# Decode attention with a dense branch: the last head's output weights in two halves of the width, the sum in two banks

## The chip, the cores and the metric

One core of a Trainium2 chip. The metric is device time in microseconds (us). "Before" and "changed" are the two kernels.

In the lines of the profile, PE is the tensor engine (matmuls) and PEld its weight loads, DVE is VectorE, ACT ScalarE, POOL GpSimd, and SPq the queue of SyncE, which issues the transfers. A line of the timeline gives start and length in us, the engine, the line of the kernel and the operation; in brackets stand the idle time before it and what ended it. PSUM is the memory that matmuls write their sums to; a bank is one part of it. A transfer has landed when the last of its completion signals (16 for a load here) is recorded.

## The reference

Two branches are added to a residual: attention of 16 query heads over the last 4096 positions of a key and value cache of 8 heads, with an output projection, and a small dense layer.

```python
W = min(4096, max(256, Sk // 4))                 # 4096
q = (layernorm(x) @ wq)...                        # B=2, one position, 16 heads of 256
k = repeat(k_cache[:, :, Sk-W:, :], 2)            # 8 kv heads -> 16
scores = einsum("bhqd,bhkd->bhqk", q, k) * 256**-0.5
o = einsum("bhqk,bhkd->bhqd", softmax(scores), v)
return x + o.reshape(B, 1, 4096) @ wo + dense(layernorm(x))   # [2, 1, 448]
```

The cache slices and the weights make 77.66 MB. The arithmetic is small: the result is 2 rows of 448 values.

## The kernel before

The key and value caches stream in through one DMA queue, issued by SyncE. Each kv head's two query heads end in matmuls with 448 KB of output weights. The weights of the last kv head (query heads 14 and 15, 224 KB each) are the last thing loaded. From there on the sum lives in four column tiles of one PSUM bank, 112 columns each:

```python
NO, DO = 4, D // 4                                 # 4 pieces of 112 columns
psA = ps_a.tile([P, DO], FP32, name="psA")         # one bank; piece n in partitions 32n, 32n+1
def add_last(lhsT, w, start=False, stop=False):
    for n in range(NO):
        nc.tensor.matmul(part(n), lhsT=lhsT, rhs=w[:, n*DO:(n+1)*DO], tile_position=(0, n*Q), ...)
...
# loads of the last weights: one transfer per query head, rows of 1792 bytes per partition
win = A_wo[r0 : r0 + rep*Dh, :].rearrange("(h p c) d -> p h (c d)", h=rep, p=P)
...
for h in range(rep):                               # the last kv head
    for c in range(ND):                            # ND = 2 halves of the head's 256 values
        add_last(oT[:, c, h, :], w[:, h, c*D:(c+1)*D], ...)
...
for n in range(NO):                                # the end
    copy = nc.vector.tensor_copy if n // 2 == 0 else nc.scalar.copy
    copy(out=res[:, n*DO:(n+1)*DO], in_=part(n))
nc.sync.dma_start(out=out, in_=res[:])
```

The softmax here doesn't subtract the row's maximum and nothing guards it: scores larger than these inputs give would overflow.

Of the kernel before, what the change touches and what calls it, by code (L numbers as in the profile page):

```python
# [12 lines left out]
FP32 = mybir.dt.float32  # L13
# [21 lines left out]
def kernel(  # L35
# [13 lines left out]
    nc = tc.nc  # L49
    P = 128  # L50
    Q = 32
    NQ = P // Q

    Bsz, Sq, D = A_x.shape
    _, Hkv, Sk, Dh = A_k_cache.shape
    HqDh = A_wq.shape[1]
    Hq = HqDh // Dh
    rep = Hq // Hkv
# [14 lines left out]
    ND = Dh // P  # L73
# [21 lines left out]
    ps_a = ctx.enter_context(tc.tile_pool(name="ps_a", bufs=1, space=PSUM))  # L95
# [16 lines left out]
    for lo, hi in ((0, SC), (SC, NS)):  # L112
# [16 lines left out]
        out=rstd[:], in_=mv[:, 1:2], func=ACT.Sqrt, bias=eps_t[:], scale=1.0  # L129
# [5 lines left out]
    for r in range(2):  # L135
        n = (NS + 1 - r) // 2
        nc.vector.tensor_scalar(  # L137
            out=xn_bf[:, r : NS : 2, :, :],
# [12 lines left out]
    for j in range(1, NQ):  # L151
        nc.vector.tensor_tensor(
            out=hsel, in0=hsel, in1=ident[:, j * Q : (j + 1) * Q : HS], op=ALU.add
# [4 lines left out]
    for b in range(Bsz):  # L158
        nc.vector.tensor_reduce(
            out=off[:, b : b + 1], in_=hsel[:, b * rep : (b + 1) * rep], axis=AXIS.X, op=ALU.add  # L160
# [4 lines left out]
        out=off[:], in0=off[:], scalar1=mine[:], scalar2=1e4, op0=ALU.subtract, op1=ALU.mult  # L165
# [4 lines left out]
    for h in range(rep):  # L170
        nc.vector.tensor_reduce(
            out=own[:, :, h],
            in_=ident[:, h * PH : (h + 1) * PH].unsqueeze(1).to_broadcast([P, Bsz, PH]),
# [14 lines left out]
    for s in range(NS):  # L188
# [7 lines left out]
        out=odd[:],  # L196
        in_=ident[:].rearrange("p (u o) -> p o u", o=2),
# [4 lines left out]
    for par in range(2):  # L202
        for x in range(NX):
            which = (par + x) % 2
            nc.vector.tensor_scalar(
                out=xs[:, par : NS : 2, x, :],
# [3 lines left out]
                op0=ALU.mult,  # L210
            )

    psE = ps_a.tile([Bsz, D], FP32, name="psE")

    def add(lhsT, w, start=False, stop=False):
        nc.tensor.matmul(  # L216
            psE[:], lhsT=lhsT, rhs=w, start=start, stop=stop, skip_group_check=True
        )
# [2 lines left out]



    NO = NQ
    DO = D // NO
    psA = ps_a.tile([P, DO], FP32, name="psA")

    def part(n):
        return psA[n * Q : n * Q + Bsz, :]

    def add_last(lhsT, w, start=False, stop=False):
        for n in range(NO):
            nc.tensor.matmul(  # L233
                part(n),
                lhsT=lhsT,
                rhs=w[:, n * DO : (n + 1) * DO],
                start=start,
                stop=stop,
                tile_position=(0, n * Q),
                skip_group_check=True,  # L240
            )

    def carry():
        early = consts.tile([Bsz, D], FP32, name="early")
        nc.vector.tensor_copy(out=early[:], in_=psE[:])
        add_last(ident_f[0:Bsz, 0:Bsz], early[:, :], start=True)


# [29 lines left out]
    def build_q(i):  # L278
# [17 lines left out]
    nc.vector.tensor_copy(  # L296
        out=half[:], in_=ident[0:NX, 0:NX].unsqueeze(2).to_broadcast([NX, NX, Bsz])
    )
    NB1 = 5
    act_bf = consts.tile([P, NF, NX, Bsz], BF16)  # L300
    dense = {}

    def load_dense():
# [14 lines left out]
        b1_in = B_b1.rearrange("(x f) -> x f", x=NX)  # L318
        for u in range(NB1):
            cols = slice(u * HF // NB1, (u + 1) * HF // NB1)  # L320
            nc.scalar.dma_start(out=b1_sb[:, cols], in_=b1_in[:, cols])
# [59 lines left out]
    def load_k(i, cuts=(0, T)):  # L381
        k_t[i] = k_pool.tile([P, T * Dh], BF16, tag="k", name="k")
        load_cache(k_t[i], A_k_cache, i, cuts)

    def load_v(i, cuts=(0, T)):
        t = v_tile()
        load_cache(t, A_v_cache, i, cuts)
        v_t[i] = t[:].rearrange("p (t d) -> p t d", t=T)

    def load_wo(kvh, parts=1):  # L390
        w = wo_pool.tile([P, rep, ND * D], BF16, tag="wo", name="wo")
        r0 = kvh * rep * Dh
        wo_t[kvh] = w
        if kvh < Hkv - NFIX:

            nc.sync.dma_start(
                out=w[:].rearrange("p h n -> p (h n)"),
                in_=A_wo[r0 : r0 + rep * Dh, :].rearrange("(p j) d -> p (j d)", p=P),
            )
            return  # L400
        win = A_wo[r0 : r0 + rep * Dh, :].rearrange("(h p c) d -> p h (c d)", h=rep, p=P)
        for u in range(parts):
            hs = slice(u * rep // parts, (u + 1) * rep // parts)
            nc.sync.dma_start(out=w[:, hs, :], in_=win[:, hs, :])  # L404

    def turn(s):
        kt = kt_pool.tile([P, TH * Dh], BF16, tag="kt", name="kt")
        i, half = divmod(s, NH)
        k = k_t[i] if half < NH - 1 else k_t.pop(i)
        nc.vector.transpose(  # L410
            out=kt[:].bitcast(FP32),
            in_=k[:, half * TH * Dh : (half + 1) * TH * Dh].bitcast(FP32),
        )
        kt_t[s] = kt
# [31 lines left out]
    def turn_p(s):  # L446
        pT = p_pool.tile([P, TH * Q], BF16, tag="pT", name="pT", bufs=2 * NH + 1)
        nc.vector.transpose(out=pT[:], in_=p_t.pop(s)[:])  # L448
        pT_t[s] = pT
        i, half = divmod(s, NH)  # L450
        if half != NH - 1:
            return
        rs = state.pop(("rs", i))
        total = small.tile([P, 1], FP32, tag="total", name="total")
        nc.vector.tensor_reduce(out=total[:], in_=rs[:], axis=AXIS.XY, op=ALU.add)
        sums = small.tile([P, BR], FP32, tag="sums", name="sums")
        nc.vector.tensor_scalar(  # L457
            out=sums[:], in0=hsel, scalar1=total[:], scalar2=None, op0=ALU.mult
        )
        state["sums", i] = sums  # L460
# [75 lines left out]
    def finish(i):  # L536
        pqv = state.pop(("pq", i))
        rec = state.pop(("rec", i))

        o = small.tile([P, NJ, NP, BR], FP32, tag="osum", name="osum")  # L540
        for u in range(NP):
            nc.vector.tensor_tensor(
                out=o[:, :, u, :],
                in0=pqv[:, :, u, u * BR : (u + 1) * BR],
                in1=rec[:].unsqueeze(1).to_broadcast([P, NJ, BR]),
                op=ALU.mult,
            )
        oT = small.tile([P, NJ, Bsz], BF16, tag="oTm", name="oTm")
        with nc.allow_low_precision("sums of fp32 factors, rounded once"):
            nc.vector.tensor_reduce(  # L550
                out=oT[:],
                in_=o[:].rearrange("p j u (b h) -> p j b u h", b=Bsz),
                axis=AXIS.XY,
                op=ALU.add,
            )
        state["oT", i] = oT
# [22 lines left out]
    def mix(kvh):  # L579
        oT = state.pop(("oT", kvh))  # L580
        w = wo_t.pop(kvh)
        if kvh < Hkv - NFIX:
            for j in range(NJ):
                add(
                    oT[:, j, :],
                    w[:].rearrange("p h (c d) -> p (h c) d", c=ND)[:, j, :],
                    stop=(kvh == Hkv - NFIX - 1 and j == NJ - 1),
                )
            return
        for h in range(rep):  # L590
            for c in range(ND):
                add_last(
                    oT[:, c, h, :],
                    w[:, h, c * D : (c + 1) * D],
                    stop=(kvh == Hkv - 1 and h == rep - 1 and c == ND - 1),
                )

    load_k(0)
    load_dense()
# [4 lines left out]
    for i in range(Hkv + 1):  # L604
        if i + 1 < Hkv:
            load_k(i + 1, (0, T) if i + 1 < Hkv - 1 else (0, T // 2, T))
        if i < Hkv:
            load_v(i, (0, T) if i < Hkv - 1 else (0, T // 2, 13 * T // 16, 15 * T // 16, T))
            load_wo(i, parts=1 if i < Hkv - 1 else 2)
            for piece in range(NH):  # L610
                s = i * NH + piece
                if s + 1 < NSTEP:
                    turn(s + 1)
                if piece == 1 and i > 1:
                    finish(i - 2)
                scores(s)
                if i == Hkv - 1 and piece == 2:
                    carry()
                if s >= 1:
                    turn_p(s - 1)  # L620
                if s == NSTEP - 1:
                    turn_p(s)
                if piece == 0 and i > 1:
                    turn_o(i - 2)
                if piece == 1 and i > 1:
                    mix(i - 2)
            if i + 2 < Hkv:
                build_q(i + 2)
        else:
            mix(i - 2)  # L630
        if i == 0:
            dense_in()
            dense_out()
        if i >= 1:
            if i - 1 < Hkv - NFIX:
                values(i - 1)
            else:
                values_fixed(i - 1)
        if i == Hkv:
            mix(i - 1)  # L640

    res = consts.tile([Bsz, D], BF16)
    for n in range(NO):
        copy = nc.vector.tensor_copy if n // 2 == 0 else nc.scalar.copy
        copy(out=res[:, n * DO : (n + 1) * DO], in_=part(n))
    nc.sync.dma_start(out=out.flatten_outer_dims(), in_=res[:])
    issue_in_order(tc)
# [30 lines left out]
```

## Time and profile before

| | before |
|---|---|
| median of the first 3 runs | 189.32 us (189.31 to 189.41) |
| load queue busy | 97.0% of the span |
| PE / VectorE / ScalarE busy | 75% / 58% / 24% |
| last weights at PE | 184.56 us |
| store issued | 185.56 us |
| span of the profile | 187.6 us |

The span is counted from the first instruction profiled; the device time of that run, 189.44 us, is 1.9 us longer. Read the table from below: the store leaves 2 us before the end, the last weights reach PE 1 us before the store, and up to about 183 us the loads have kept the memory busy; then they run dry. The lines of the profile are in the prediction.

### The profile page before, as it was taken

The numbers are of one execution on the slowest core, as the hardware profiler recorded it, in microseconds if no ns is written. First come the engines' busy times: TensorE is split into PE (matmuls) and PEld (weight loads), VectorE is DVE, ScalarE is ACT, GpSimd is POOL, SyncE is SP. The second block draws the span as 40 slices with busy tenths as digits, with TensorE's granted clock in tenths as the row PEclk, the third lists the DMA queues.
The fourth block names the chain that finished last, engine by engine and source line by source line (L and its number), as shares of the span: only waits on it lengthen the run. The fifth ranks groups of instructions, "written<-read, shape, count | busy, mean of one in ns | idle before, by whom it ended". The sixth has DMA issues, their size and how long they took to land.

```text
span 187.6 us, 2418 instructions
## 1 busy us (share of the span) xinstructions
PE 140.9 (75%) x938; PEld 64.9 (35%) x938; DVE 108.6 (58%) x150; ACT 45.3 (24%) x148; POOL 16.3 (9%) x74
## 2 busy tenths in 40 slices
PE   0394099904989999956896769955995869999773
PEld 0141033801334434422342324421441324444672
DVE  6705497049671994079803992099506993995201
ACT  3005015200062144024222224033312233154001
POOL 7000500300003001100030003000120000000000
PEclk9999859965799999999999999999999999999655
DMA  6999899999999999999998999999999999999991
GB/s 228 414 477 440 378 429 444 447 444 447 433 419 426 407 420 445 433 447 390 484 446 384 426 433 440 433 447 421 446 437 426 390 438 426 451 444 398 415 395 43
DMA packets 5046, 77.81 MB, mean 415 GB/s; under 512 B 552, under 2 KB 1068, under 8 KB 2348
## 3 DMA queue, kind: packets, MB, share of 16 engines
q1 hardware_dynamic: 5012, 77.66, 97.0%
q8 instruction: 7, 0.11, 0.2%
q14 instruction: 3, 0.02, 0.0%
q10 hardware_dynamic: 24, 0.01, 0.0%
HBM read 77.67 MB, written 0.00 MB: 414 GB/s over the span
## 4 chain that ended last, share of the span: by engine, by line
DMA 66%; DVE 20%; PE 8%; SPq 2%; ACT 1%; issue 1%; ACTq 0%; DVEq 0%
DMA k<-in_A_k_cache_dram 57%; DVE kt L410 16%; DMA wo<-in_A_wo_dram 9%; PE sc L422 4%; PE o L490 4%; DVE pT L448 3%; SPq L379 2%; ACT p L436 1%; PE psE L216 0%; SPq L113 0%; DVE sums L457 0%; SPq L404 0%; DVE oTm L550 0%; DVE recm L482 0%; PE psA L233 0%
## 5 line engine op out<-in xcount | busy, mean ns | idle before, releaser
L410 DVE STREAM_TRANSPOSE kt<-k 128x2048 f32<-128x2048 f32 x32 | 73.3, 2295 | 51.8 <-DMA k<-in_A_k_cache_dram 51.8
L422 PE MATMUL sc<-kt,qdiag 128*128 128x512 bf16 x256 | 62.6, 389 | 19.7 <-DVE kt L410 18.9
L436 ACT ACTIVATE p<-sc,off 128x256 bf16<-128x256 f32 x64 | 33.0, 543 | 69.6 <-PE sc L422 69.0
L490 PE MATMUL o<-v,pT 128*8 128x512 bf16 x192 | 42.5, 379 | 0.0
L422 PEld LDWEIGHTS <-qdiag 128*128 128x128 bf16 x256 | 23.0, 98 | 55.7 <-issue 20.9
L490 PEld LDWEIGHTS <-pT 128*8 128x8 bf16 x192 | 17.2, 92 | 22.4
L448 DVE STREAM_TRANSPOSE pT<-p 128x512 bf16<-128x512 bf16 x32 | 21.8, 681 | 5.1 <-ACT p L436 5.1
L285 POOL COPY qdiag<-qt 32x16 bf16<-32x16 bf16 x64 | 12.9, 247 | 120.2 <-PE sc L422 104.2
L499 ACT COPY o_sb<-o 8x512 f32<-8x512 f32 x12 | 6.3, 572 | 36.3 <-PE o L490 36.3
L436 ACT ACTIVATION_READ_ACCUMULATOR p<-sc,off 128x1 f32 x64 | 11.7, 183 | 0.0
L216 PE MATMUL psE<-wo,oTm 128*2 128x448 bf16 x24 | 5.5, 351 | 6.5 <-DVE oTm L550 6.5
L216 PE MATMUL psE<-v,act_bf 128*2 128x448 bf16 x14 | 4.9, 533 | 7.0 <-DVE act_bf L360 7.0
L569 PE MATMUL q<-pT,v 128*128 128x4 bf16 x256 | 7.8, 169 | 2.4 <-DMA v<-in_A_v_cache_dram 2.1
L265 PE MATMUL q_ps<-v,xq 128*128 128x512 bf16 x28 | 7.5, 435 | 2.1 <-DVE xq L256 2.1
L569 PEld LDWEIGHTS <-v 128*128 128x128 bf16 x256 | 7.3, 101 | 3.4 <-DMA v<-in_A_v_cache_dram 3.3
L275 DVE CAST q_sb<-q_ps 128x512 bf16<-128x512 f32 x2 | 1.3, 686 | 7.0 <-PE q_ps L265 7.0
L265 PEld LDWEIGHTS <-xq 128*128 128x128 bf16 x28 | 3.0, 110 | 6.6 <-DVE xq L256 2.5
L216 PEld LDWEIGHTS <-oTm 128*2 128x2 bf16 x24 | 1.5, 82 | 10.7 <-DVE oTm L550 9.0
L216 PEld LDWEIGHTS <-act_bf 128*2 128x2 bf16 x14 | 1.6, 117 | 10.0 <-DVE act_bf L360 7.1
L189 PE MATMUL xnT_ps<-ident,xn_bf 2*128 2x2 bf16 x7 | 0.5, 166 | 5.7 <-DVE xn_bf L137 5.7
L529 PEld LDWEIGHTS q<-ident_f,o_sb 8*128 8x128 f32 x48 | 3.4, 136 | 2.5 <-issue 2.5
L529 PE MATMUL q<-ident_f,o_sb 8*128 8x8 f32 x48 | 3.9, 204 | 0.0
(60 smaller groups left out, 46.5 us busy)
## 6 DMA issues: line engine op xcount, KB each, us to landing
k<-in_A_k_cache_dram SPq DMA_DIRECT2D x7, 4096.0 KB, 26.9
v<-in_A_v_cache_dram SPq DMA_DIRECT2D x7, 4096.0 KB, 25.7
k<-in_A_k_cache_dram SPq DMA_DIRECT2D x2, 2048.0 KB, 28.8
v<-in_B_w_dram SPq DMA_DIRECT2D x2, 1568.0 KB, 17.0
wo<-in_A_wo_dram SPq DMA_DIRECT2D x7, 448.0 KB, 30.2
v<-in_A_wq_dram SPq DMA_DIRECT2D x1, 2048.0 KB, 7.4
v<-in_A_v_cache_dram SPq DMA_DIRECT2D x1, 2048.0 KB, 15.2
v<-in_A_wq_dram SPq DMA_DIRECT2D x1, 1536.0 KB, 10.8
```

The source lines that it names most:

```text
L216: nc.tensor.matmul(psE[:], lhsT=lhsT, rhs=w, start=start, stop=stop, skip_group_check=True)
L265: nc.tensor.matmul(ps[u][:], lhsT=xq[:, s, :, :].rearrange("p j k -> p (j k)"), rhs=wq_sb[:, s, u * N5 : (u + 1) * N5], start=(s == 0), st ...
L285: nc.gpsimd.tensor_copy(out=tv[rows, :, e, j * Q : (j + 1) * Q : HS].rearrange("p n (b h) -> p n b h", b=Bsz), in_=qv[rows, :, h0 : h0 + r ...
L379: nc.sync.dma_start(out=t[:, cols], in_=src[:, :, cols])
L410: nc.vector.transpose(out=kt[:].bitcast(FP32), in_=k[:, half * TH * Dh : (half + 1) * TH * Dh].bitcast(FP32),)
L422: nc.tensor.matmul(psc[:], lhsT=qdiag[i % NW][:, n * NE + e, :], rhs=ktv[:, n, e, :, :], start=(n == 0 and e == 0), stop=(n == NB - 1 and ...
L436: nc.scalar.activation(out=pv[:, b, :, :], in_=sv[:, b, :, :], func=ACT.Exp, scale=scale, bias=off[:, b : b + 1], accum_out=state["rs", i] ...
L448: nc.vector.transpose(out=pT[:], in_=p_t.pop(s)[:])
L490: nc.tensor.matmul(po[:], lhsT=pT_t[i * NH + piece][:, uh * NP * Q : (uh + 1) * NP * Q : HS], rhs=v[:, u * NP : (u + 1) * NP, :].rearrange ...
L499: nc.scalar.copy(out=o_sb[:, u, :, :, :], in_=po[:, u * Dh : (u + 1) * Dh] .rearrange("r (m j) -> r j m", j=NJ) .unsqueeze(2) .to_broadcas ...
L529: nc.tensor.transpose(pqv[:, j, u, :], o_sb[:, u, j, :, :].rearrange("r h m -> r (h m)"), ident_f[0:NR, 0:NR],)
L569: nc.tensor.matmul(po[:, c, :], lhsT=vv[:, t, c, :], rhs=pTv[:, th, 0:Q:HS], start=(t == 0 and c == 0), stop=(t == T - 1), skip_group_chec ...
```

## The change

Intent: have half of the result finished and copied out while the second half of the last head's weights (224 KB in all) is still landing, so that only one copy per engine is left at the end. The cut diff:

```diff
+    banks = []
     def part(n):
-        return psA[n * Q : n * Q + Bsz, :]
+        return banks[2 * n // NO][n * Q : n * Q + Bsz, :]
 ...  (in carry(), after the early sum was copied out of psE)
+        for tag in ("a", "e"):
+            banks.append(ps_a.tile([P, DO], FP32, tag=tag, name="psA"))
 ...
-    NB1 = 5
+    NB1 = 4                                  # pieces in which a bias is loaded
 ...  (loads of the last kv head)
+        nc.sync.dma_start(out=w[:, 0 : rep - 1, :], in_=win[:, 0 : rep - 1, :])
+        for x in range(2):
+            cols = slice(x * D // 2, (x + 1) * D // 2)      # runs of 448 bytes
+            nc.sync.dma_start(out=w[:, rep - 1, :]...[:, :, cols], in_=win[:, rep - 1, :]...[:, :, cols])
 ...  (matmuls)
+            last = kvh == Hkv - 1 and h == rep - 1
+            for parts in (range(NO // 2), range(NO // 2, NO)) if last else (range(NO),):
+                for c in range(ND):
+                    add_last(oT[:, c, h, :], w[:, h, c*D:(c+1)*D], stop=(last and c == ND - 1), parts=parts)
 ...  (the end)
-        copy = nc.vector.tensor_copy if n // 2 == 0 else nc.scalar.copy
+        copy = nc.vector.tensor_copy if n % 2 == 0 else nc.scalar.copy
```

More of the change, by code (lines that the diff above doesn't have):

```diff
@@ L211 @@
             )
-    psE = ps_a.tile([Bsz, D], FP32, name="psE")
+    psE = ps_a.tile([Bsz, D], FP32, tag="e", name="psE")
     def add(lhsT, w, start=False, stop=False):
@@ L225, with add_last @@
     DO = D // NO
-    psA = ps_a.tile([P, DO], FP32, name="psA")
+    banks = []
     def part(n):
-        return psA[n * Q : n * Q + Bsz, :]
-    def add_last(lhsT, w, start=False, stop=False):
-        for n in range(NO):
+        return banks[2 * n // NO][n * Q : n * Q + Bsz, :]
+    def add_last(lhsT, w, start=False, stop=False, parts=range(NO)):
+        for n in parts:
             nc.tensor.matmul(
@@ L388, in load_v, with load_wo @@
         v_t[i] = t[:].rearrange("p (t d) -> p t d", t=T)
-    def load_wo(kvh, parts=1):
+    def load_wo(kvh):
         w = wo_pool.tile([P, rep, ND * D], BF16, tag="wo", name="wo")
@@ L401, in load_wo @@
         win = A_wo[r0 : r0 + rep * Dh, :].rearrange("(h p c) d -> p h (c d)", h=rep, p=P)
-        for u in range(parts):
-            hs = slice(u * rep // parts, (u + 1) * rep // parts)
-            nc.sync.dma_start(out=w[:, hs, :], in_=win[:, hs, :])
+        if kvh < Hkv - 1:
+            nc.sync.dma_start(out=w[:], in_=win)
+            return
+        nc.sync.dma_start(out=w[:, 0 : rep - 1, :], in_=win[:, 0 : rep - 1, :])
+        for x in range(2):
+            cols = slice(x * D // 2, (x + 1) * D // 2)
+            nc.sync.dma_start(
+                out=w[:, rep - 1, :].rearrange("p (c d) -> p c d", c=ND)[:, :, cols],
+                in_=win[:, rep - 1, :].rearrange("p (c d) -> p c d", c=ND)[:, :, cols],
+            )
     def turn(s):
@@ L590, in mix @@
         for h in range(rep):
-            for c in range(ND):
-                add_last(
-                    oT[:, c, h, :],
-                    w[:, h, c * D : (c + 1) * D],
-                    stop=(kvh == Hkv - 1 and h == rep - 1 and c == ND - 1),
-                )
+            last = kvh == Hkv - 1 and h == rep - 1
+            for parts in (range(NO // 2), range(NO // 2, NO)) if last else (range(NO),):
+                for c in range(ND):
+                    add_last(
+                        oT[:, c, h, :],
+                        w[:, h, c * D : (c + 1) * D],
+                        stop=(last and c == ND - 1),
+                        parts=parts,
+                    )
     load_k(0)
@@ L608 @@
             load_v(i, (0, T) if i < Hkv - 1 else (0, T // 2, 13 * T // 16, 15 * T // 16, T))
-            load_wo(i, parts=1 if i < Hkv - 1 else 2)
+            load_wo(i)
             for piece in range(NH):
```

## The prediction

> **What bounds the kernel now.** I read the page first, then the chain of waits for its last 27 us, then the stretches and the order of instructions at the very end, and last the records of single DMA packets in the trace. From the page:
>
> ```profile
> PE 140.9 (75%) x938; PEld 64.9 (35%) x938; DVE 108.6 (58%) x150; ACT 45.3 (24%) x148; POOL 16.3 (9%) x74
> ...
> DMA  6999899999999999999998999999999999999991
> ...
> q1 hardware_dynamic: 5012, 77.66, 97.0%
> ```
>
> No compute engine is above 75%, while the load queue keeps the 16 DMA engines busy for 97% of the span; every slice but the first and last is at 8 or 9. The 77.66 MB of cache and weights set the time. Nothing in the change removes a byte, so it can only work on what follows the last byte. The end of the chain of waits:
>
> ```profile
> 167.25 17.26 DMA wo<-in_A_wo_dram
> 184.51 0.04 issue
> 184.56 0.46 PE psA L233 x7
> 185.02 0.23 ACT res L645
> 185.25 0.27 ACTq L673
> ```
>
> The reader is to see that the last thing awaited is the second transfer of the last output weights (head 15's 224 KB). It was issued at 167.25 and queued behind the value cache, so an issue more on SyncE costs nothing. The instructions of the end in order of time:
>
> ```profile
> 183.48 0.37 PE L569 MATMUL q<-pT,v 128*128 128x4 bf16 x8
> 183.89 0.17 DVE L511 TENSOR_TENSOR oT<-q,rec 128x8 bf16<-128x8 f32 x1 [2.86 <-PE q L569]
> ...
> 184.11 0.80 PE L233 MATMUL psA<-wo,oT 128*2 128x112 bf16 x16 [0.26 <-DVE oT L511]
> ...
> 184.94 0.56 DVE L645 CAST res<-psA 2x112 bf16<-2x112 f32 x2 [0.88 <-PE psA L233]
> 185.01 0.52 ACT L645 CAST res<-psA 2x112 bf16<-2x112 f32 x2 [11.46 <-PE psA L233]
> 185.56 0.33 SPq L646 DMA_DIRECT2D out_dram<-res  x1
> ```
>
> Eight of the sixteen matmuls (head 14) run at 184.11. The other eight wait for the last weights until 184.56, and the last of them ends at 184.91. Then each of two engines makes two copies, one after the other, and the store is issued at 185.56. So from the last weights at PE to the store there is 1.00 us, and after the store 187.6 - 185.56 = 2.0 us that the change does not touch. The stretches say when the loads run dry:
>
> ```profile
> 182.00:183.00 1.00, 0.99 (x37) 0.91 (x35) 0.00 (x0) 0.00 (x0) 0.00 (x0) 0.50 0.91 344
> 183.00:183.50 0.50, 0.38 (x15) 0.29 (x13) 0.00 (x0) 0.00 (x0) 0.00 (x0) 0.50 0.50 191
> 183.50:184.00 0.50, 0.36 (x8) 0.27 (x8) 0.11 (x1) 0.00 (x0) 0.00 (x0) 0.50 0.37 140
> 184.00:184.50 0.50, 0.36 (x8) 0.18 (x9) 0.06 (x1) 0.00 (x0) 0.00 (x0) 0.50 0.04 14
> ```
>
> Columns are busy times, granted clock, DMA share and GB/s. The DMA share falls in steps: the sixteen engines do not end together, and the slowest one alone decides when the last weights are there. In the packet records its last 8 packets of 1792 bytes start at 183.669 and follow each other every 70.6 ns; its completion write is at 184.234, and PE starts 0.32 us after that. Before them the same engine brought head 14's 8 packets, done at 183.664.
>
> **What the Trainium skill says.** "DMA: Bandwidth & Descriptors", Specifications, gives 512 bytes as the smallest transfer for line rate, with a read-modify-write below it. The new pieces are 448 bytes. The trace of before has few packets below that: the bias rows of 358 bytes took 22 ns each. A line through 1792 bytes (74 ns), 2048 (84 ns) and 4096 (159 ns) gives 8 + 0.037 x 358 = 21 ns there, so no penalty is visible; but those were lone packets, not a row of them. The same page, "How a descriptor splits into AXI transactions", says that a piece that does not start on a 256-byte boundary is fetched from the boundary below, the rest unused. In before each row is 1792 bytes and starts on one; of the four new pieces of a row three do not. No packet here shows the price. "VectorE: DVE Perf Modes", section on the TRN2 errata, gives copies from PSUM as 120 + FD cycles on VectorE and 172 + FD on ScalarE; for 112 elements that is 242 and 237 ns, and the trace has 262 and 245. Nearly all is fixed cost, so two copies in turn cost twice one. "TensorEngine Tiling (Array Packing)", Key Properties, says that tiles run in parallel. The trace agrees: the last eight matmuls of about 0.25 to 0.30 us each take 0.36 us together, so half as many save little.
>
> **The change part by part.**
>
> 1. *Copies.* Before, both engines copy two pieces after the last matmul: ScalarE from 185.01 to 185.52. Now the sum's first half (pieces 0 and 1) lies in its own bank and is complete first; VectorE and ScalarE copy one piece of it each while the second half is still awaited, then one piece each of the second half. If the first half's two copies are out of the way, the end holds one copy per engine: 0.27 us less on ScalarE (185.276 - 185.007, the distance of its two starts). They are out of the way if the first half's weights reach PE some 0.35 us before the second's, worked out in 3.
>
> 2. *Matmuls after the last weights.* Eight become four, on two column tiles. Their starts lie 2 to 4 ns apart and the second weight row's start 0.05 us after the first's; the chain is still two deep. From 0.355 us to about 0.345: 0.01 saved. Sum of 1 and 2: the store comes about 0.72 to 0.73 us after PE sees the last weights, in place of 1.00. Gain 0.28 us.
>
> 3. *The transfers.* Head 15's 128 rows of 1792 bytes become two transfers of 256 pieces of 448 bytes. Each of the 16 engines has 32 small packets for 8 long ones. Distances between packet starts on one engine: 70.6 ns for 1792 bytes, 80.2 for 2048, so 0.0375 ns per byte and some 3 ns per packet: 448 bytes take 20 ns. 32 x 20 = 646 against 8 x 70.6 = 565 ns: 0.08 us more, with one more completion write 0.09. If unaligned starts are fetched as the skill says, a row's 56 beats of 32 bytes become 68 (14, 20, 18 and 16 for the four pieces); 12 x 8 rows at 70.6/60 = 1.18 ns each is an estimate of 0.11 us more, so 0.20. If small packets do not overlap and cost their full line duration, 8 + 0.037 x 448 = 25 ns plus waste, it is 0.25 to 0.35. If the sub-512 penalty doubles the 20 ns, 0.73. I take 0.23. The first half then lands at about 183.669 + 16 x 25 = 184.07 and the second at about 184.46; PE sees them at 184.39 and 184.78. The first copies run at about 184.8 to 185.05, and the second half's matmuls end at 185.13: the copies are hidden, just.
>
> 4. *The rest.* Carrying the early sum over uses the old bank again for the second half; the matmul that does so needs the copy of that bank anyway, and it is done long before the end. The bias is brought in four pieces for five: one issue of 0.27 us less on ScalarE's queue at 4 to 6 us, before it has work. It keeps the number of transfers constant, and with it the turn of the completion semaphores at the end; at the start two weight loads may wait for an earlier partner and issue sooner (they were issued at 8.16 and 11.97 us), but the first key block, issued at 1.65, keeps the queue full until 20.8. The third weight transfer at the end probably waits for the value block of the turn before, which lands at 172.5; the queue is then full for another 10 us. None of this is on the path: 0.
>
> Sum: -0.28 + 0.23 = -0.05 us. Time 189.32 - 0.05, rounded to 189.25.
>
> **The rivals.**
>
> *The transfer is free.* If the 448-byte pieces cost only what the straight line says, the last weights come 0.09 us later and the gain is 0.19: 189.13. For it: the 358-byte bias rows are on the line.
>
> *The small packets eat the gain and more.* With the sub-512 penalty the last landing is 0.73 later: 189.32 + 0.73 - 0.28 = 189.77. For it: the skill's figure; the slowest engine has no slack, so each nanosecond of it counts. Against it: the lone 358-byte packets at 22 ns.
>
> *The first half's copies are in the way.* If the two halves land within less than 0.3 us of each other, the second copies wait for the first, and a part of the 0.28 is lost. In the straight-line case the halves are 0.33 apart, so this would cost 0.05 at the most. It belongs with cheap packets and so eats into the first rival's gain.
>
> *The slowest engine is another.* A 16 KB instruction fetch runs on the engines at 182.57, for 0.88 us. Where such a fetch falls moves the last landing by some tenths either way, and nothing in the change governs it.
>
> **Range and chances.** The rivals span 189.1 to 189.8, the three runs of before 0.1, and the fetches and the DMA's own scatter some tenths. Predicted 189.25 us, range 188.8 to 189.8. Two per cent is 3.8 us, more than the whole 3.0 us after the last weights at PE: faster 0.01, within 2% 0.975, slower 0.015.
>
> **What would show it.** In the changed profile: packets of 448 bytes about 25 ns apart on the slowest engine (20 and 40 mark the rivals); the last four matmuls starting 0.2 to 0.3 us later after the loads than now; the first copy of each engine ending before the last matmul; one copy of 0.25 us between the last matmul and the store, so 0.73 us from those matmuls' start to the store. Wrong would be a first half that reaches PE no earlier than the second, a change of DMA share before 180 us, or a store later by more than 0.5 us.

## The result, and the profile after

| | before | changed |
|---|---|---|
| median of 6 runs | 189.37 us (189.31 to 189.44) | 189.19 us (189.06 to 189.41) |
| ratio | | 0.9992, interval 0.9979 to 1.0005 |
| span of the profile | 187.6 us | 187.6 us |

The times alone say "the same". The changed kernel's run that was profiled took 189.39 us, one of its two slowest, and before's took 189.44 us, its slowest of six, so the traces must be compared piece by piece and not by their ends. First the page's lines on loads, which answer to the busy shares of before:

```profile
DMA packets 5442, 77.81 MB, mean 415 GB/s; under 512 B 1076, under 2 KB 1464, under 8 KB 2744
...
q1 hardware_dynamic: 5412, 77.66, 97.2%
```

The bytes are the same and the busy share is hardly more (97.2% for 97.0%); the queue has 400 more packets. That is 512 new ones of 448 bytes for 128 rows and 16 more completion writes. Then the instructions of the end:

```profile
184.29 0.93 PE L234 MATMUL psA<-wo,oT 128*2 128x112 bf16 x16 [0.26 <-DVE oT L522]
184.88 0.09 PEld L234 LDWEIGHTS <-oT 128*2 128x2 bf16 x3 [0.23 <-issue]
184.94 0.58 DVE L659 CAST res<-psA 2x112 bf16<-2x112 f32 x2 [0.70 <-PE psA L234]
184.98 0.56 ACT L659 CAST res<-psA 2x112 bf16<-2x112 f32 x2 [10.77 <-PE psA L234]
185.59 0.34 SPq L660 DMA_DIRECT2D out_dram<-res  x1
```

The second line marks the last four matmuls, which the second half of the weights releases at 184.88. The copies begin at 184.94 and 184.98, while those matmuls still run (the last ends at 185.23): the first half of the sum leaves under them. From 184.88 to the store at 185.59 are 0.71 us, where before had 1.00. And the stretches:

```profile
183.00:183.50 0.50, 0.50 (x16) 0.49 (x16) 0.00 (x0) 0.00 (x0) 0.00 (x0) 0.50 0.62 212
183.50:184.00 0.50, 0.42 (x11) 0.30 (x8) 0.00 (x0) 0.00 (x0) 0.00 (x0) 0.50 0.43 126
184.00:184.50 0.50, 0.24 (x10) 0.18 (x9) 0.17 (x1) 0.00 (x0) 0.00 (x0) 0.50 0.21 58
```

The last two columns are DMA share and GB/s. In the last of these stretches the loads still have a share of 0.21, where before was down to 0.04: the last weights land later. In 183.5 to 184 a busy share of 0.43 carries 126 GB/s, where before carried 140 with 0.37: that is what small packets look like.

To compare runs whose loads end at different moments, the trace's records of completions are of more use. The last value block (256 KB) comes just ahead of the weights and is the same in every kernel. (These records stand in the trace, but no view of the profile prints them.) All times in us from the start of each span:

```
kernel              last value   last weights  store    weights after  store after  store after
                    block lands  land          issued   value block    weights      value block
before              183.437      184.514       185.559  1.077          1.045        2.12
changed             183.603      184.834       185.593  1.231          0.759        1.99
again               183.597      184.836       185.59   1.239          0.754        1.99
copies_only         183.525      184.619       185.67   1.094          1.051        2.15
split_only          183.714      184.941       185.90   1.227          0.959        2.19
before_two_copies   183.388      184.476       185.23   1.088          0.754        1.84
one_bank            183.438      184.661       185.42   1.223          0.759        1.98
nb5                 183.448      184.692       185.45   1.244          0.758        2.00
quarters            183.526      184.935       185.631  1.409          0.696        2.11
h0_tiny             183.341      185.893       186.650  2.552          0.757        3.31
wide                183.376      184.459       185.51   1.083          1.051        2.13
transposed          183.438      184.528       186.11   1.090          1.58         2.67
```

In the first two rows: the weights land 0.15 us later after the value block, the store follows the weights 0.29 us sooner, and 0.13 us remain. The value block itself lands anywhere from 183.34 to 183.71 in this table, in kernels that differ ahead of it only in the bias load and in when two early weight loads are issued. That scatter of nearly 0.4 us is larger than what the change can gain. It does not come from the end: the first half of the last key block lands at 157.85 to 158.20, and from there to the value block it is 25.47 to 25.52 us in all twelve traces. The scatter arises before 158 us; what makes it there, these traces do not say.

### The profile page after: what moved, and what is told of

Read it like the earlier page. It is cut to its first block, busy times and chain, and to the rows that moved or that the text cites. A ratio compares the mean times of both kernels' runs of the same rounds, so it can differ in the third digit from the quotient of the medians.

```text
span 187.6 us, 2417 instructions
## 1 busy us (share of the span) xinstructions
PE 148.5 (79%) x938; PEld 67.5 (36%) x938; DVE 108.6 (58%) x150; ACT 45.3 (24%) x148; POOL 16.3 (9%) x74
## 3 DMA queue, kind: packets, MB, share of 16 engines
q1 hardware_dynamic: 5412, 77.66, 97.2%
## 4 chain that ended last, share of the span: by engine, by line
DMA 66%; DVE 17%; PE 13%; SPq 2%; ACT 1%; issue 1%; DVEq 0%
DMA k<-in_A_k_cache_dram 57%; DVE kt L421 13%; DMA v<-in_A_v_cache_dram 9%; PE sc L433 7%; PE o L501 4%; DVE pT L459 2%; SPq L382 1%; PE psE L216 1%; ACT p L447 1%; PE psA L234 1%; PE q L540 1%; SPq L113 0%; DVE sums L468 0%; PE q L580 0%; DVE oTm L561 0%
## 5 line engine op out<-in xcount | busy, mean ns | idle before, releaser
L433 PE MATMUL sc<-kt,qdiag 128*128 128x512 bf16 x256 | 67.5, 414 | 16.8 <-DVE kt L421 16.5
L433 PEld LDWEIGHTS <-qdiag 128*128 128x128 bf16 x256 | 24.1, 101 | 55.3 <-issue 25.4
L216 PE MATMUL psE<-v,act_bf 128*2 128x448 bf16 x14 | 5.4, 574 | 6.6 <-DVE act_bf L363 6.6
L268 PE MATMUL q_ps<-v,xq 128*128 128x512 bf16 x28 | 8.3, 468 | 2.1 <-DVE xq L259 2.1
L216 PE MATMUL psE<-wo,oTm 128*2 128x448 bf16 x24 | 6.4, 398 | 3.1 <-DVE oTm L561 3.1
L540 PEld LDWEIGHTS q<-ident_f,o_sb 8*128 8x128 f32 x48 | 4.1, 162 | 3.4 <-issue 3.4
L540 PE MATMUL q<-ident_f,o_sb 8*128 8x8 f32 x48 | 4.7, 220 | 0.0
## 6 DMA issues: line engine op xcount, KB each, us to landing
wo<-in_A_wo_dram SPq DMA_DIRECT2D x7, 448.0 KB, 25.4
```

What stands on the lines that cost most here:

```text
L216: nc.tensor.matmul(psE[:], lhsT=lhsT, rhs=w, start=start, stop=stop, skip_group_check=True)
L268: nc.tensor.matmul(ps[u][:], lhsT=xq[:, s, :, :].rearrange("p j k -> p (j k)"), rhs=wq_sb[:, s, u * N5 : (u + 1) * N5], start=(s == 0), st ...
L433: nc.tensor.matmul(psc[:], lhsT=qdiag[i % NW][:, n * NE + e, :], rhs=ktv[:, n, e, :, :], start=(n == 0 and e == 0), stop=(n == NB - 1 and ...
L540: nc.tensor.transpose(pqv[:, j, u, :], o_sb[:, u, j, :, :].rearrange("r h m -> r (h m)"), ident_f[0:NR, 0:NR],)
```

## The experiments

Theory: the gain is one copy per engine, 0.29 us; 0.15 us of it is paid back by the small packets. Rivals: the 0.18 us between the medians is scatter; or the banks alone, the order of copies alone, or the changed start of the kernel makes it.

### again: the changed kernel once more

No edit.

> The changed kernel once more, unaltered, to narrow the ratio. Theory (the wait from last weights at PE to the store shrinks from 1.00 to 0.72 us, the small packets give 0.10 to 0.12 back): 0.17 us less than before, ratio 0.9991. Rival (the 0.18 us seen is scatter of the slowest DMA engine): ratio 1.0000 within 0.0003.

Measured: 189.38 us (189.09 to 189.46) against 189.33 (189.2 to 189.65), ratio 0.9999, interval 0.9986 to 1.0012. The time lies nearer to the rival's 1.0000 than to the theory's 0.9991 and excludes neither; the runs scatter too much. The row in the table repeats the first trace to 0.01 us in each of the three distances. So the mechanism is steady and the clock time isn't a fine enough instrument for it. From here on the distances decide, and the times only guard against something outside of them.

### copies_only: banks, order and crossing without the split transfer

"Crossed" means that each engine copies one piece of each half.

```diff
-        nc.sync.dma_start(out=w[:, 0 : rep - 1, :], ...)
-        for x in range(2): ...            # two halves of the width
+        for h in range(rep):
+            nc.sync.dma_start(out=w[:, h : h + 1, :], in_=win[:, h : h + 1, :])
-    NB1 = 4
+    NB1 = 5
```

> Two banks, the matmuls by halves and the crossed copies, but the last head's weights in one transfer of whole rows, the bias in five. Theory: both halves of the sum become ready some 0.01 to 0.05 us apart, so each engine's second copy still queues behind its first: about 1.0 us from the last weights at PE to the store, time of before within 0.05 us. Rival (banks and the crossing alone give the gain): 0.72 us and 0.28 us less.

Measured: 189.41 us, ratio 1.0001 (0.9987 to 1.0014). The timeline of its end:

```profile
184.66 0.10 PEld L234 LDWEIGHTS <-oT 128*2 128x2 bf16 x7 [0.28 <-issue]
185.04 0.56 DVE L654 CAST res<-psA 2x112 bf16<-2x112 f32 x2 [0.89 <-PE psA L234]
185.08 0.51 ACT L654 CAST res<-psA 2x112 bf16<-2x112 f32 x2 [10.95 <-PE psA L234]
185.67 0.33 SPq L655 DMA_DIRECT2D out_dram<-res  x1
```

From the last weights at PE to the store 1.01 us, as in before: both copies of each engine come after the matmuls. Two banks and the new order give nothing while all weights land at once. The rival falls.

### split_only: the split transfer with the old dealing of copies

```diff
-        copy = nc.vector.tensor_copy if n % 2 == 0 else nc.scalar.copy
+        copy = nc.vector.tensor_copy if n // 2 == 0 else nc.scalar.copy
```

> The changed kernel with the copies dealt as before (VectorE both pieces of the first half, ScalarE both of the second). Theory: ScalarE again has two copies after the last matmul, so 0.99 us from the last weights at PE to the store; with the small packets' 0.11 on top, 0.10 us slower than before and 0.27 slower than the changed kernel. Rival (the split of the weights itself gives the gain): as fast as the changed kernel.

Measured: 189.48 us (189.45 to 189.68), ratio 1.001 (0.9998 to 1.0023).

```profile
184.99 0.09 PEld L234 LDWEIGHTS <-oT 128*2 128x2 bf16 x3 [0.24 <-issue]
185.04 0.56 DVE L659 CAST res<-psA 2x112 bf16<-2x112 f32 x2 [0.70 <-PE psA L234]
185.37 0.51 ACT L659 CAST res<-psA 2x112 bf16<-2x112 f32 x2 [11.58 <-PE psA L234]
185.90 0.33 SPq L660 DMA_DIRECT2D out_dram<-res  x1
```

VectorE does both its copies early and is idle at the end; ScalarE starts at 185.37 and has two to make. The weights land 1.23 us after the value block, as in the changed kernel, and the store follows 0.96 us after them, 0.20 more than there (0.27 was expected; ScalarE's first copy starts 0.38 us after the last matmuls begin, and before's started 0.45 after). Store after value block: 2.19, the worst of before, changed, copies_only and this. Split transfer and crossed copies are worth something only together.

### before_two_copies: the gain without its price

```diff
+        nc.vector.tensor_copy(out=res[:], in_=early[:])     # in carry(): res is filled once, early
 ...
-    for n in range(NO):
+    for n in (0, 2):
```

> The kernel before with one of each engine's two copies taken away from the end (half the result is wrong on purpose: those columns hold the sum without the last two heads). Whole-row packets. Theory: the full 0.27 us of one copy without any price for packets: 189.10, ratio 0.9986. Rival (the end is not on the path that sets the time, or the second copy was hidden): ratio 1.0000.

Measured: 189.20 us (189.0 to 189.34), ratio 0.9991 (0.9978 to 1.0003). Half the columns lack the last heads; the comparison with the reference passed all the same, so the tolerance doesn't see that part. The store comes 0.754 us after the weights, the changed kernel's 0.759, while the weights land as early as in before. The time alone, with an interval up to 1.0003, decides nothing; the distances do. This is the whole of what one copy per engine is worth: 2.12 - 1.84 = 0.28 us. The changed kernel has 0.13 of it.

### one_bank: is the second bank needed?

```diff
-        return banks[2 * n // NO][n * Q : n * Q + Bsz, :]
+        return banks[0][n * Q : n * Q + Bsz, :]
 ...  (one bank is made in carry() in place of two)
```

> The changed kernel with all four pieces of the sum in one bank. Theory A (order is kept by the piece of the bank that is written or read): tail as in the changed kernel, 0.72 us from the last weights at PE to the store. Theory B (order is kept by the bank): the second half's matmuls wait for the first half's copies, or the copies for all matmuls, and the store comes 0.2 to 0.3 us later after the last weights, 0.95 to 1.0 us.

Measured: correct, 189.22 us (189.1 to 189.53), ratio 0.9996 (0.9984 to 1.0009), and a row like the changed kernel's (0.759 and 1.98).

```profile
184.12 0.93 PE L234 MATMUL psA<-wo,oT 128*2 128x112 bf16 x16 [0.26 <-DVE oT L521]
184.77 0.58 DVE L658 CAST res<-psA 2x112 bf16<-2x112 f32 x2 [0.70 <-PE psA L234]
184.81 0.56 ACT L658 CAST res<-psA 2x112 bf16<-2x112 f32 x2 [11.31 <-PE psA L234]
```

Theory A holds: the copies of the first half, from 184.77 and 184.81, run while PE writes the second half in the same bank until 185.05. "PSUM — Partial Sum Buffer", section on bank collisions, says that engines may access one bank at the same time in different quadrants of 32 partitions. The pieces lie in different quadrants, and this run agrees. The two banks of the change cost nothing and gain nothing.

### nb5: the bias in five pieces

```diff
-    NB1 = 4
+    NB1 = 5
```

> The changed kernel with the bias in five pieces as before. Theory (off the path): tail as in the changed kernel, time within 0.1 us of it; the two early weight loads issue at 8.2 and 12.0 us again in place of 2.3 and 8.3. Rival (their earlier issue costs the load queue something): the last value block of 256 KB lands at 183.4 as before in place of 183.6, and the time is 0.15 us lower.

Measured: 189.33 us (189.29 to 189.35), ratio 0.9999 (0.9985 to 1.0013). The issues of SyncE's first microseconds, first in this run, then in the changed kernel:

```profile
1.65 0.62 SPq L382 DMA_DIRECT2D k<-in_A_k_cache_dram  x1
8.02 0.33 SPq L309 DMA_DIRECT2D v<-in_B_w_dram  x1
11.86 0.38 SPq L316 DMA_DIRECT2D v<-in_B_w_dram  x1
```

```profile
1.66 0.62 SPq L382 DMA_DIRECT2D k<-in_A_k_cache_dram  x1
2.33 0.58 SPq L309 DMA_DIRECT2D v<-in_B_w_dram  x1
8.35 0.38 SPq L316 DMA_DIRECT2D v<-in_B_w_dram  x1
```

The dense weights (the two lines of B_w) are issued 3.5 and 5.7 us later again, as in before. The end is that of the changed kernel (0.758 and 2.00). The value block landed at 183.45 as the rival asked, but it did so at 183.44 in one_bank too, which has four pieces. That does not settle it. Of the four traces with four pieces the other three land at 183.60 to 183.71, and of the six with five pieces none lands later than 183.53. The times (189.33 us here, 189.22 and 189.38 us with four pieces) show no cost of the early issues, but a cost of some 0.1 us is neither shown nor excluded; if there is one, it comes off the 0.13 us.

### quarters: twice as many packets, half as large

```diff
-        for x in range(2):                 # halves; matmuls by halves
+        for x in range(4):                 # quarters, runs of 224 bytes; matmuls by quarters
-    NB1 = 4
+    NB1 = 2
```

> The last head's weights in four quarters of the width, 224-byte pieces, matmuls by quarters, copies crossed, bias in two pieces. Theory: 64 packets of 11 ns per engine, 0.72 us, plus four completions: last weights 0.67 to 0.75 us after the head before (0.65 in the changed kernel, 0.52 in before), and the end holds two matmuls and ScalarE's one copy, so the same 0.72 us to the store: within 0.1 us of the changed kernel. Rival (a packet has a floor of 20 ns): 1.3 us after the head before, 0.6 us slower.

Measured: 189.72 us (189.67 to 189.85), ratio 1.0021 (1.0007 to 1.0035). The weights landed 1.41 us after the value block, 0.18 later than in the changed kernel; from the head before, 0.84 us. Expected were 0.67 to 0.75, the rival had 1.3: between them, near the theory. In the packet records 224-byte packets follow each other every 13.0 ns on an engine (11 expected); 64 x 13.0 = 0.83 us, which is the distance measured. The store follows the weights in 0.70 us, so store after value block is 2.11, 0.12 worse than the changed kernel. The time is 0.4 to 0.5 us worse than that of nb5 and one_bank (189.33 and 189.22 us), which have the changed kernel's end and ran in the same rounds. Part of that is outside the span: the profiled run took 2.05 us more than its span, where before took 1.88 and the changed kernel 1.79 more. Where those 0.2 to 0.3 us go, no profile here shows.

### h0_tiny: 112-byte packets

```diff
-        nc.sync.dma_start(out=w[:, 0 : rep - 1, :], in_=win[:, 0 : rep - 1, :])
+        for x in range(2):                 # head 14 in interleaved blocks of 56 columns
+            nc.sync.dma_start(out=w[:, 0, :].rearrange("p (j x d) -> p x j d", x=2, j=8)[:, x], ...)
-    NB1 = 4
+    NB1 = 3
```

> The changed kernel with the weights of the head before the last (224 KB) in pieces of 112 bytes, two interleaved transfers, the bias in three: 128 packets per DMA engine for 8. Theory (a packet costs about 3 ns and 0.0375 ns per byte, also below 512 bytes): 7 ns each, 909 against 565 ns, the last weights 0.35 us later than in the changed kernel, measured from the landing of the last value block: that distance was 1.23 us and becomes 1.58. Rival (small packets have a floor as of the 358-byte rows, 16 to 22 ns): 1.5 to 2.2 us later.

Measured: 190.90 us (190.63 to 191.13), ratio 1.0084 (1.0069 to 1.01). Neither theory: the last weights landed 2.55 us after the value block (183.341 and 185.893). But the two tiny transfers themselves were done at 184.536, 1.20 us after it. Whole rows need 0.56 there (183.437 to 183.994 in before), so 120 packets more per engine cost 0.64 us, 5 ns each; they follow each other every 9.4 ns (7 expected). The rest is something else, seen in SyncE's own queue:

```profile
166.48 1.32 SPq L410 DMA_DIRECT2D wo<-in_A_wo_dram  x2
172.39 11.56 SPq L416 DMA_DIRECT2D wo<-in_A_wo_dram  x2
```

The two tiny transfers (2048 pieces) are issued in 1.32 us. The first half of head 15 then holds SyncE for 10.86 us of the 11.56, and the second can be issued only at 183.30. Both come when a part of the DMA engines has run out of work (the first packet of 448 bytes starts at 184.04, the last of 112 bytes at 184.20):

```profile
183.50:184.00 0.50, 0.26 (x8) 0.17 (x7) 0.17 (x1) 0.00 (x0) 0.00 (x0) 0.50 0.49 67
184.00:184.50 0.50, 0.00 (x0) 0.00 (x0) 0.00 (x0) 0.00 (x0) 0.00 (x0) 0.50 0.75 159
184.50:185.00 0.50, 0.33 (x8) 0.20 (x9) 0.00 (x0) 0.00 (x0) 0.00 (x0) 0.50 0.51 117
```

The share falls to 0.49, rises to 0.75 when new work comes, and falls again. That an issue waits because the queue holds only so many pieces is the likely reading; the trace shows the wait, not its cause. The changed kernel stays clear of it: its three weight issues take 0.56 to 0.59 us each. In quarters the third and fourth quarter's issues took 3.06 and 1.42 us.

### wide: one copy per engine without small packets

```diff
-    NO = NQ
+    NO = 2                                 # from the kernel before: two pieces of 224 columns
-        copy = nc.vector.tensor_copy if n // 2 == 0 else nc.scalar.copy
+        copy = nc.vector.tensor_copy if n == 0 else nc.scalar.copy
```

> The kernel before with the sum in two pieces of 224 columns in place of four of 112: one copy per engine, no small packets, one bank. Theory (copies are mostly fixed cost, packets cost 4.7 ns each): one copy of 0.34 to 0.38 us for two of 0.25, and 0.09 us more for the wider matmuls at half clock; 0.91 us from the landing of the last weights to the store (1.045 in before, 0.76 in the changed kernel), and the last weights 1.08 us after the last value block as in before: together 1.99 us, as good as the changed kernel (1.99) and 0.13 better than before (2.12). Rival (a copy's time goes with its width): no gain over before.

Measured: 189.30 us (189.2 to 189.3) against 189.36, ratio 0.9994 (0.998 to 1.0007). The theory missed:

```profile
184.50 0.09 PEld L233 LDWEIGHTS <-oT 128*2 128x2 bf16 x3 [0.18 <-issue]
185.07 0.38 DVE L645 CAST res<-psA 2x224 bf16<-2x224 f32 x1 [1.06 <-PE psA L233]
185.10 0.34 ACT L645 CAST res<-psA 2x224 bf16<-2x224 f32 x1 [11.49 <-PE psA L233]
185.51 0.33 SPq L646 DMA_DIRECT2D out_dram<-res  x1
```

The copies take 0.38 and 0.34 as expected, but the first can start only 0.57 us after the last matmuls begin, where before needed 0.38. Half as many column tiles, twice as wide, cost 0.18 us at the half clock granted there, not 0.09, and that is all that the saved copies gave. Store after value block: 2.13, as in before.

### transposed: weights stationary, one copy of 8 values per partition

```diff
-                part(n), lhsT=lhsT, rhs=w[:, n * DO : (n + 1) * DO],
+                psA[:, n, :], lhsT=w.rearrange("p (q n) -> p n q", n=NO)[:, n, :], rhs=lhsT,
-    four copies and a store of 2 rows
+    nc.vector.tensor_copy(out=res[:].rearrange("p b n -> p n b"), in_=psA[:])
+    nc.sync.dma_start(out=out...rearrange("b (q n) -> q b n", n=NO), in_=res[:])   # 8-byte pieces
```

> The kernel before with the last two heads' product turned round: weights stationary, four columns blocks of 112 partitions by 2, so that one VectorE copy of 8 elements per partition ends it; whole-row packets; the store in 224 pieces of 8 bytes. Theory: eight weight loads at 27 ns as in the value stage, 0.38 us, one copy of 0.17, 0.67 us from the landing of the last weights to the store and 1.75 us from the last value block; but the store's many pieces cost 0.1 to 0.2 us after that: 0.1 to 0.25 us faster than before in all. Rival (tiny stores of 8 bytes are dear): the store lands over 0.4 us later than before's 1.15 us after issue and the gain is gone.

Measured: 192.26 us (192.04 to 192.67), ratio 1.0155 (1.0141 to 1.0169), clearly slower, for two reasons.

```profile
184.12 1.75 PE L230 MATMUL psA<-oT,wo 128*112 128x2 bf16 x16 [0.26 <-DVE oT L507]
185.91 0.17 DVE L639 CAST res<-psA 112x8 bf16<-112x8 f32 x1 [1.84 <-PE psA L230]
186.11 0.35 SPq L640 DMA_DIRECT2D out_dram<-res  x1
```

The one copy is as cheap as hoped (0.17 us). But sixteen weight loads of 112 columns follow each other every 104 ns, and not every 27 ns as the value stage's loads of 128 columns do. "TensorE: Matmul & The Clock Gate", section on weight-path modes, says that the fast weight load needs 128 columns; the two distances agree with that. They do not isolate it: the loads here also take every fourth column of the weights, those of the value stage every second. And the store in 8-byte pieces landed 3.36 us after its issue (186.107 to 189.472), where before's two rows of 896 bytes needed 1.15 (185.559 to 186.709). The rival was right.

## Why the prediction was right

*The time.* Predicted 189.25 us and "within 2%"; measured 189.19, and 189.38 when run again. Both lie in the range, but so would a time with no change at all: the range of 0.5 us to each side is wider than anything in dispute, and that the middle fell within 0.15 us of both is partly luck. The mechanism has to be judged by its terms. The four kernels with the same end (changed, again, nb5, one_bank) have ratios of 0.9992, 0.9999, 0.9999 and 0.9996, each compatible with no change at all; the mean, 0.9997, stands for some 0.07 us. The 0.13 us of the traces are shown as a mechanism, not as a time.

*Step 1, copies:* right. Predicted gain with step 2 0.28 us; measured 1.045 - 0.759 = 0.29. The run without the second copies reaches the same 0.754. The first copies are hidden "just", as the prediction said: VectorE and ScalarE have 0.05 and 0.07 us between their two copies. The halves reach PE 0.315 us apart, predicted 0.35 to 0.39.

*Step 2, matmuls:* right. The last four start at 184.877 and end at 185.226, 0.35 us.

*Step 3, the transfers:* right in kind, too large in size. The prediction took 0.23 us from a spread of 0.09 to 0.73; 0.15 was measured (1.231 - 1.077), and 0.15 to 0.17 in the runs with the same transfers. The packet records give its parts (they do not name the engine; packets at a constant distance are taken for one engine's): 448-byte packets every 21.2 ns, so 32 x 21.2 - 8 x 70.6 = 113 ns, and 6 ns for the second completion. Of the remaining 0.03 us, 0.02 lie between the slowest engine's last completion write and the semaphore (0.28 in before, 0.30 in the changed kernel). No run split the weights into two transfers without small packets, so this rest is not assigned. The straight line's 20 ns was nearly right, and the extra cost for unaligned starts, the full duration of 25 ns per packet and the doubling below 512 bytes didn't appear. (The estimate for unaligned starts divides 70.6 ns by 60 beats, though it counts 56 in a row; that makes 0.11 us of 0.12 and changes nothing.) The line itself was too low at its foot: 13.0 ns at 224 and 9.4 at 112 bytes put the fixed part nearer to 5 ns than to 3, which is why quarters came out 0.1 us dearer than expected of it.

*Step 4, the rest:* nothing speaks against it, but it is not shown for the early issues: nb5's time shows no cost, and the landings leave some 0.1 us open. The third weight transfer did wait, as said, for the value block of the turn before (issued at 172.64), without effect.

*The rivals.* The free transfer came closest: it put the gain at 0.19 us, and the distances say 0.13. The sub-512 penalty, 40 ns for a packet, is refuted for these loads by the 21.2 ns. The first half's copies were not in the way: each engine stood idle before its second copy. "The slowest engine is another" was right that something outside of the change moves the last landing by some tenths, but not about the place. The instruction fetch starts at 182.42 to 183.06 us in the twelve traces, while the value block follows the last key block steadily (25.47 to 25.52 us) and the weights follow the value block within 0.02 us in kernels with the same transfers. The scatter comes from before 158 us. That it makes the spread of the times is likely, and argued rather than shown.

## What to carry to other kernels

When the loads bound a kernel to its last byte, count what follows that byte: here one microsecond, of which a second copy per engine was 0.28. To hide such a copy, the last transfer must be split so that its first part lands at least one copy's time earlier, and what the split costs in small packets comes straight off the gain, because the slowest DMA engine has no slack. Measure it as distances in the trace from a common event; run times that scatter by 0.3 us can't tell 0.13 us. And look how far back a scatter goes before blaming the end for it.

## What the Trainium skill lacked or had wrong

- "DMA: Bandwidth & Descriptors", Specifications, sets 512 bytes as the smallest transfer for line rate. For loads into on-chip memory these runs show a smooth decline and no sign of a step between 1792 and 448 bytes: packets on one engine follow each other every 70.6 ns (1792 bytes), 21.2 (448), 13.0 (224) and 9.4 (112), close to 5 ns plus 0.037 ns per byte, that is 25.4 bytes per ns at 1792 and 21.1 at 448. The store in 8-byte pieces was slow: 3.36 us to landing against 1.15.
- Same page, "How a descriptor splits into AXI transactions": the beats of unaligned starts cost no visible time. The 448-byte pieces start at four different offsets from a 256-byte boundary, and rows of 16 packets on one engine start 21 to 22 ns apart throughout.
- How many pieces may be queued before an issue on SyncE is held back, no page that I found says; "Perfetto Trace Analysis" speaks of a descriptor buffer that fills, without a size. Here an issue took 10.86 us behind 2048 pieces of 112 bytes.
